# A pooled-attention and token-mixing kernel: the second batch's q transposed by transfers instead of TensorE, and alpha2 multiplied behind the transposes

## The chip, the cores and the metric

The kernel runs on one core of a Trainium2 chip. A core has TensorE (PE in the profile: matrix products and transposes by a product with the identity), VectorE (DVE), ScalarE (ACT), GpSimd (POOL) and SyncE (SP), which work through their own instruction streams and wait for each other by semaphores, and 16 engines for transfers. The metric is the device time of one execution in microseconds. Transfers issued by GpSimd appear in the profile as queue q0, those of SyncE as q1.

## What is computed

The inputs are q, k and v of 8 batches, 8 heads, 576 rows and 64 columns, all float32. First an attention in which k and v are averaged over groups of 8 rows, so that each of the 576 queries sees 72 keys:

```python
k_p = k.reshape(B, H, Sp, pool, D).mean(axis=3)      # 576 rows -> 72
v_p = v.reshape(B, H, Sp, pool, D).mean(axis=3)
scores = scale * np.matmul(q, k_p.transpose(0, 1, 3, 2))
attn = softmax(scores)
x = np.matmul(attn, v_p)          # heads side by side: (8, 576, 512)
```

Then a block that mixes rows and then columns:

```python
a1 = alpha1 * x + beta1
tok = np.einsum('ts,bsd->btd', w_tok, a1)
u = x + lam * tok
a2 = alpha2 * u + beta2
ch = np.maximum(a2 @ w_ch1, 0.0) @ w_ch2             # 512 -> 2048 -> 512
out = u + lam * ch
```

## The kernel before

The eight batches go through a software pipeline. Each batch has 576 rows, cut into four chunks of 128 and a rest of 64; the rests of two batches make one chunk together, so there are 36 chunks, worked on in nine blocks of four. While block n is in the two large products (`mlp_A`, L849, and from the third block on `product`, L972), the attention and the row mixing of batch n + 1 run between them.

The order of the work is written by hand. For batch 0 and the first half of block 0 the calls simply stand in their order (from L994 on). From then on every piece of a block has a due time in a list, `todo`, which is sorted (L1205) and emitted in that order; all engines get their instructions in the order of emission. There is no scheduler behind it.

The steps that matter here:

- **Warm-up.** `keep_warm` (L788) issues matrix products of zeros, 13 of 512 columns at L999, before q of batch 0 has landed.
- **q transposed.** The scores need q with the head's columns on the partitions. `att_F` (L575) makes two tiles `qT` per batch, one for heads 0 to 3 and one for heads 4 to 7. For batches 0 and 1 it does so on TensorE, four transposes of 128x128 (L589) for each half tile, and a copy out of PSUM (L596). From batch 2 on it is one transposing transfer per tile, issued by SyncE (L584). `att_S4` (L689) reads the tiles: the first group of four heads reads `qT[0]`, the second `qT[1]`.
- **Loads of batch 1.** q of batch 1 (`load_q_bf`), k (`load_k`, issued by GpSimd for this batch), the weights `w_ch1` in three pieces (`load_w1`), v (`load_v32`, tiles `v_main` and `v_rest`) and `w_ch2` in four pieces (`load_w2`) all go through GpSimd's queue in the first 40 us. `sum_v` (L316) adds up v on VectorE, `first_V` (L651) reads the sums.
- **Row mixing.** `mix_T` (L794) makes five products for a chunk, adds x on VectorE (L805), giving `u`, and makes a bf16 copy `u_bf`. For batch 0 this copy is multiplied by alpha2, spread over all partitions in `al2_bc` (L811, by GpSimd for chunks 0 and 2 and by VectorE for 1 and 3). For later batches it is a cast on ScalarE (L809), as alpha2 has been multiplied into `w_ch1` by then.
- **Spread alpha2.** `load_al2` (L484, called at L1032) loads alpha2 to all 128 partitions through SyncE's queue, 256 KB.
- **u transposed.** `mix_uT` (L813) transposes `u_bf` of block 0 on TensorE (L825) and copies it out of PSUM on ScalarE (L827) into `u_fm[0]`; later blocks use transposing transfers (L820).
- **First product.** For block 0, `mlp_A` (L849) runs in two halves of 256 rows: the first half needs chunks 0 and 1, the second half chunks 2 and 3.
- **Row sums.** `setup_rowsum` (L522) makes five products that put the sums of the rows of `w_tok` where beta1 needs them; the fifth call stands at L1182 with due time 6.2.

## Time and profile before

| | us |
|---|---|
| median of three runs | 332.82 (332.25 to 332.84) |
| the profiled execution | 332.3 |
| its span, first to last instruction | 330.6 |
| TensorE busy | 324.9 (98%) |
| VectorE busy | 235.5 (71%) |
| ScalarE busy | 175.5 (53%) |
| GpSimd busy | 95.6 (29%) |

The page's fourth part follows the work that ended last back to the start, and gives the share of each engine and line. Its fifth part lists groups of instructions: line, engine, operation, what it writes and reads, the shape, how many, then busy time and mean duration, then the idle time of the engine ahead of them and what ended it. The timeline has the same, in order of time: start, duration, engine, line. In a group of pipelined matrix products the sum of durations is more than the time they take, and the chain shows how far they advance. The transfer view gives, for each queue, packets, megabytes and the time that the packets took as a share of the 16 engines, which can be above 100% where packets overlap. TensorE is at its granted clock of 1.000 over the whole span.

### The profile page before, as it was taken

To read this page: it belongs to the slowest core of one execution; us is meant where nothing else is said; L and a number is where in the kernel's file an instruction comes from. 1 tells how busy PE (TensorE), PEld (TensorE's weight loads), DVE (VectorE), ACT (ScalarE), POOL (GpSimd) and SP (SyncE) were. 2 spreads that over 40 slices of the span, in tenths; PEclk is the share of its full clock that TensorE was granted. 3 is DMA by queue.
4 is the path that set the end of the run, shared out by engine and by line. 5 is a ranking of instruction groups with operands and counts; after the bars stand their busy time and mean duration, and the time that the engine had idled before them with its cause. 6 is when DMAs were issued, how large, how long until landed. Compare 5 with 4: busy or idle time off the path is not lost.

```text
span 330.6 us, 6522 instructions
## 1 busy us (share of the span) xinstructions
PE 324.9 (98%) x2528; PEld 208.9 (63%) x2528; DVE 235.5 (71%) x490; ACT 175.5 (53%) x322; POOL 95.6 (29%) x110
## 2 busy tenths in 40 slices
PE   8999999999999999999999999999999999999995
PEld 3667764455545576656775677557755866586584
DVE  6674389999589969776967796878688783265263
ACT  2775989458323852387128812782268225803710
POOL 8769738301256011700290028102610200000000
PEclk9999999999999999999999999999999999999999
DMA  8999999959894982499549934995340044003003
GB/s 119 193 219 270 268 210 249 207 145 124 165 255 68 221 203 59 76 227 165 164 119 201 171 125 89 207 195 157 65 136 2 0 65 143 2 0 129 2 32 97
DMA packets 66618, 45.83 MB, mean 139 GB/s; under 512 B 34541, under 2 KB 57205, under 8 KB 66586
## 3 DMA queue, kind: packets, MB, share of 16 engines
q1 hardware_dynamic: 52236, 32.67, 42.6%
q0 software_dynamic: 13824, 12.40, 22.9%
q8 instruction: 20, 0.33, 0.4%
q10 hardware_dynamic: 526, 0.34, 0.3%
q14 instruction: 12, 0.10, 0.1%
HBM read 38.30 MB, written 9.44 MB: 144 GB/s over the span
## 4 chain that ended last, share of the span: by engine, by line
PE 98%; DVE 1%; issue 0%; ACT 0%
PE ps_h L849 38%; PE ps_w L972 26%; PE ps_tok L801 12%; PE ps_ch L869 8%; PE ps_av L743 3%; PE ps_s L700 2%; PE ps_warm L792 2%; PE ps_kp L632 1%; PE ps_r L707 1%; PE ps_av L747 1%; PE ps_q L589 1%; PE ps_sc L680 0%; PE ps_rs L528 0%; PE ps_w L516 0%; PE ps_uT L825 0%; PE ps_v L659 0%
## 5 line engine op out<-in xcount | busy, mean ns | idle before, releaser
L849 PE MATMUL ps_h<-u_fm,w 128*128 128x512 bf16 (+2 forms) x608 | 133.7, 369 | 0.2 <-DVE bias_cols L852 0.2
L856 ACT ACTIVATE H<-ps_h,bias_cols 128x512 bf16<-128x512 f32 x144 | 98.1, 688 | 56.5 <-PE ps_h L849 55.5
L849 PEld LDWEIGHTS <-w 128*128 128x128 bf16 x608 | 65.8, 114 | 49.7 <-issue 2.2
L972 PEld LDWEIGHTS <-H 128*128 128x128 bf16 x560 | 53.4, 98 | 10.9 <-DVE u_sb L990 1.2
L809 ACT CAST u_bf<-u_sb 128x512 bf16<-128x512 f32 x32 | 19.8, 618 | 70.0 <-issue 39.9
L972 PE MATMUL ps_w<-w_l,H 128*128 128x256 bf16 x448 | 53.6, 273 | 0.0
L990 DVE TENSOR_TENSOR u_sb<-u_sb,ps_w 128x512 f32<-128x512 f32 x54 | 36.3, 682 | 17.0 <-PE ps_w L972 17.0
L765 POOL TENSOR_TENSOR xs<-x_tm,lamal_bc 128x512 bf16<-128x512 f32 x12 | 15.9, 1330 | 108.8 <-DVE x_tm L751 108.6
L801 PE MATMUL ps_tok<-xs,wtT 128*128 128x512 bf16 (+3 forms) x200 | 44.9, 381 | 0.1
L805 DVE TENSOR_TENSOR u_sb<-x_tm,ps_tok 128x512 f32<-128x512 f32 (+1 forms) x40 | 27.3, 683 | 9.9 <-PE ps_tok L801 9.9
L751 DVE TENSOR_TENSOR x_tm<-ps_av,recs 128x320 f32<-128x320 f32 x64 | 31.5, 492 | 2.6
L729 ACT ACTIVATE ET<-ps_s 72x512 f16<-72x512 f32 x56 | 32.3, 591 | 0.0
L801 PEld LDWEIGHTS <-wtT 128*128 128x128 bf16 (+3 forms) x200 | 17.4, 100 | 16.2 <-issue 1.1
L749 DVE RECIPROCAL recs<-ps_av 128x5 f32<-128x5 f32 x64 | 12.1, 188 | 16.7 <-PE ps_av L747 16.6
L670 DVE TENSOR_TENSOR v_u<-v_u 72x1024 f32<-72x1024 f32 (+1 forms) x24 | 22.7, 948 | 0.2
L972 PE MATMUL ps_w<-w_t,h_s 128*128 128x256 bf16 x168 | 22.6, 273 | 0.0
L869 PEld LDWEIGHTS <-H 128*128 128x128 bf16 x128 | 11.9, 98 | 13.7 <-issue 0.4
L372 POOL TENSOR_TENSOR k_raw<-k_raw 128x512 f32<-128x512 f32 x14 | 18.7, 1338 | 1.2 <-PE ps_ch L869 0.7
L972 PEld LDWEIGHTS <-h_s 128*128 128x128 bf16 x168 | 16.4, 98 | 4.1
L941 DVE TENSOR_TENSOR H<-H,H 128x1024 bf16<-128x1024 bf16 x14 | 9.7, 690 | 12.8 <-ACT H L856 12.7
L374 POOL TENSOR_TENSOR k_bf<-k_raw 128x512 bf16<-128x512 f32 x14 | 18.5, 1318 | 1.1
L743 PEld LDWEIGHTS <-ET 72*128 72x128 f16 x256 | 14.0, 97 | 6.0 <-DVE vp L664 0.3
(153 smaller groups left out, 369.3 us busy)
## 6 DMA issues: line engine op xcount, KB each, us to landing
out_dram<-u_sb SPq DMA_DIRECT2D x29, 256.0 KB
k_raw<-in_k_dram SPq DMA_DIRECT2D x12, 512.0 KB
v_u<-in_v_dram SPq DMA_DIRECT2D x12, 512.0 KB
q_bf<-in_q_dram POOLq DMA_DIRECT2D x16, 256.0 KB, 7.4
w<-in_moe_w_ch_dram POOLq DMA_DIRECT2D x6, 512.0 KB, 12.9
out_dram<-u_sb SPq DMA_DIRECT2D x11, 128.0 KB
w<-in_moe_w_ch_dram POOLq DMA_DIRECT2D x1, 1024.0 KB, 14.3
k_raw<-in_k_dram POOLq DMA_DIRECT2D x2, 512.0 KB, 16.7
```

The lines of the kernel that those rows point to most:

```text
L670: nc.vector.tensor_tensor(out=out, in0=t[:, :, 0:width], in1=t[:, :, width:2 * width], op=ALU.add)
L729: nc.scalar.activation(out=o, in_=i, func=AF.Exp, bias=0.0, scale=0.125)
L743: nc.tensor.matmul(out=av[:, odd + c, :], lhsT=ET[:, m0:m0 + 128], rhs=vp1[:, h % 4, :])
L751: nc.vector.tensor_tensor(out=x[:, 1 - odd:6 - odd, dd:dd + D], in0=av[:, :, 0:64], in1=rec.unsqueeze(2).to_broadcast((P, 5, D)), op=ALU.mult)
L801: nc.tensor.matmul(out=ps_tok[p0:p1], lhsT=wtT[0:kk, at, P * c:P * c + p1 - p0], rhs=xs_pool[i][0:kk, sc, :], start=(sc == 0), stop=(sc == 4))
L805: nc.vector.tensor_tensor(out=s["u"][p0:p1, :], in0=x[p0:p1, 1 + c if c < 4 else 5 - 5 * i, :], in1=ps_tok[p0:p1, 0:DM], op=ALU.add)
L809: nc.scalar.copy(out=s["u_bf"], in_=s["u"])
L849: nc.tensor.matmul(out=ps_h[:, t0:t1 + one], lhsT=w1_of(cc, j), rhs=rhs, start=(cc == 0), stop=(cc == 3))
L856: nc.scalar.activation(out=H4[n, j // 4][:, j % 4, :], in_=ps_h, func=AF.Relu, bias=bias_cols[:, j:j + 1], scale=1.0)
L869: nc.tensor.matmul(out=ps, lhsT=H_of(n, j)[:, 128 * m:128 * m + 128], rhs=(w2l if n else w2)[j // 4][:, j % 4, :], start=(j == 0), stop=(j ...
L972: nc.tensor.matmul(out=ps, lhsT=stat(j), rhs=moving(j), stop=(j == 7), start=(first and (pp == 0 or alone) and j == 0), skip_group_check=True)
L990: nc.vector.tensor_tensor(out=o, in0=o, in1=banks[key, "both"], op=ALU.add)
```

## The change

- `att_F` uses transposing transfers from batch 1 on. The two transfers for batch 1 stand right behind `mix_T(0, 3)`; the four TensorE steps in `todo` are gone.
- `mix_T` casts `u_bf` on ScalarE for every batch. `mix_uT` multiplies by alpha2 on the way out of PSUM: chunks 0, 2 and 3 by one VectorE instruction with `al2_cols` (one value per partition and group of 128 columns), chunk 1 by four ScalarE activations of 128 columns.
- `load_al2` and the tile `al2_bc` are gone; a later tile that had used its memory gets memory of its own.
- `load_w1(1)` moves up between the two `load_k` of batch 1. `mix_uT((0, 0))` moves ahead of `setup_rowsum(3)`. `setup_rowsum(4)` moves ahead of the second halves of `mlp_A`.
- The 13 warm-up products of 512 columns become 24 of 64 columns and 9 of 512.

```diff
-        if b > 1:
+        if b:
             if r == 0:
                 nc.sync.dma_start_transpose(out=st["qT"][u],
                                             in_=st["q"][u].rearrange("p h c d -> p (h c d)"))
             return
...
-        if b:
-            nc.scalar.copy(out=s["u_bf"], in_=s["u"])
-        else:
-            eng.tensor_tensor(out=s["u_bf"], in0=s["u"], in1=al2_bc, op=ALU.mult)
+        nc.scalar.copy(out=s["u_bf"], in_=s["u"])
...
-        nc.scalar.copy(out=u_fm[blk][:, :, at // 2, 128 * (at % 2):128 * (at % 2) + 128],
-                       in_=ps_uT[:, 0:512].rearrange("p (c t) -> p c t", t=128))
+        o = u_fm[0][:, :, at // 2, 128 * (at % 2):128 * (at % 2) + 128]
+        i = ps_uT[:, 0:512].rearrange("p (c t) -> p c t", t=128)
+        if at != 1:
+            nc.vector.tensor_tensor(out=o, in0=i, op=ALU.mult,
+                                    in1=al2_cols.unsqueeze(2).to_broadcast((P, 4, 128)))
+            return
+        for cc in range(4):
+            nc.scalar.activation(out=o[:, cc], in_=i[:, cc], func=AF.Copy, bias=0.0,
+                                 scale=al2_cols[:, cc:cc + 1])
...
-    for u in range(2):
-        load_k(1, u, queue=nc.gpsimd)
-    keep_warm(13)
+    load_k(1, 0, queue=nc.gpsimd)
+    load_w1(1)
+    load_k(1, 1, queue=nc.gpsimd)
+    keep_warm(24, 64)
+    keep_warm(9)
...
-    load_al2(nc.vector)
...
-    load_w1(1)
...
-    mix_T(0, 0, nc.gpsimd)
+    mix_T(0, 0)
...
     mix_T(0, 1)
+    mix_uT((0, 0))
     setup_rowsum(3)
-    mix_T(0, 2, nc.gpsimd)
+    mix_T(0, 2)
     load_v32(1)
-    mix_uT((0, 0))
     mix_uT((0, 1))
     mix_T(0, 3)
+    att_F(1, 0)
+    att_F(1, 2)
     load_w2(0)
     load_w2(1)
...
     mlp_A(0, 3, 0, 256)
+    setup_rowsum(4)
     for j in range(4):
         mlp_A(0, j, 256, 512)
...
-            for hp in range(4):
-                todo.append((2.6 + 0.9 * hp, lambda hp=hp: att_F(b, hp)))
...
-            todo.append((6.2, lambda: setup_rowsum(4)))
```

More of the change, by code (lines that the diff above doesn't have):

```diff
@@ L388, in direct @@
     lamal_bc = const.tile([P, DM], FP, tag="lamal_bc", name="lamal_bc")
-    al2_bc = const.tile([P, DM], FP, tag="al2_bc", name="al2_bc")
     b2row = const.tile([8, P], FP, tag="b2row", name="b2row")
@@ L482, in more_constants @@
         nc.vector.memset(wtT[:, :, S:640], 0.0)
-    def load_al2(behind):
-        behind.memset(al2_bc[:, 0:1], 0.0)
-        nc.sync.dma_start(out=al2_bc, in_=moe_alpha2.unsqueeze(0).to_broadcast((P, DM)))
     def spread_lam():
@@ L786, in chunk_of, with keep_warm, mix_T @@
         return key, st2[key]
-    def keep_warm(count):
-        ps = psB.tile([P, DM], FP, tag="ch", bufs=2, name="ps_warm")
+    def keep_warm(count, n=DM):
+        ps = psB.tile([P, DM], FP, tag="ch", bufs=2, name="ps_warm")[:, 0:n]
         for _ in range(count):
-            nc.tensor.matmul(out=ps, lhsT=warm[:, 0:P], rhs=warm)
-    def mix_T(b, c, eng=nc.vector):
+            nc.tensor.matmul(out=ps, lhsT=warm[:, 0:P], rhs=warm[:, 0:n])
+    def mix_T(b, c):
         key, s = chunk_of(b, c)
@@ L917, in weight_sum @@
             wino["S2"] = [const.tile([P, 4, HALF], BF, tag=tag, name="h_s")
-                          for tag in ("early", "al2_bc")]
+                          for tag in ("early", "h_s")]
             wino["S3"] = [const.tile([P, 4, HALF], BF, tag="lam_bc", name="h_s"),
```

## The prediction, as put on record before the result was known

> **What bounds the kernel now.** I read the page's chain first, then the chain in order of time, then the timeline of the first 46 us engine by engine, then the transfers.

> ```profile
> PE 98%; DVE 1%; issue 0%; ACT 0%
> 29.56 0.17 DVE bias_cols L852
> 29.75 1.92 PE ps_h L849 x16
> 31.68 0.45 PE ps_q L589 x8
> 32.56 0.22 PE ps_q L589 x4
> 33.66 0.22 PE ps_q L589 x4
> ```

> TensorE is the chain. The q transposes of the second batch are on it: 0.45 + 0.22 + 0.22 = 0.89 us, 16 at 56 ns. A microsecond taken from TensorE is a microsecond won, unless it must wait. So I looked for what could make it wait: evictions around the first mixing, and transfers, because the changed lines load both.

> ```profile
> 23.77 1.26 POOL L811 TENSOR_TENSOR u_bf<-u_sb,al_bc 128x512 bf16<-128x512 f32 x1 [1.68 <-DMA al_bc<-in_moe_alpha_dram]
> 27.48 0.95 POOL L308 DMA_DIRECT2D v_main<-in_v_dram  x1
> 40.19 0.68 DVE L324 TENSOR_TENSOR v_main<-v_main 128x512 f32<-128x512 f32 x1
> 38.73 0.30 PE L700 MATMUL ps_s<-qT,kp 64*72 64x256 bf16 x2
> 44.33 0.30 PE L700 MATMUL ps_s<-qT,kp 64*72 64x256 bf16 x2
> ```

> These are the spread load that goes (POOL waits for it, but TensorE has other work), a load with little slack (v_main lands 12.3 us after issue, at 39.8), and the first readers of the two q tiles of the second batch, 38.7 and 44.3 us. The transposes by transfer would have to land before those. Next, the transfer view in four windows: 24 to 29 us, 26 to 46, 26 to 48, and 83.6 to 86.9, where two q transposes (SyncE, issued from 82.94) move alone; then 142.5 to 145.

> ```profile
> q0 software_dynamic: 756, 1.20, 88.9%
> q1 hardware_dynamic: 597, 0.31, 27.2%
> ...
> q0 software_dynamic: 2171, 4.92, 107.4%
> ...
> q0 software_dynamic: 2406, 5.30, 107.0%
> ...
> q1 hardware_dynamic: 2091, 0.52, 82.3%
> ...
> q0 software_dynamic: 563, 0.28, 91.0%
> q1 hardware_dynamic: 369, 0.10, 39.1%
> ```

> The columns are packets, MB and share of the 16 engines. Two q transposes are some 2,050 packets of 256 bytes and need 3 us alone. But GpSimd's queue (q0) is never empty from 5 to 54 us, and beside it SyncE's queue (q1) got 597 packets against 756: about one for one, whatever the size of q0's packets (in 27 to 28 us it is 72 against 79, and those are of 3.7 KB). So rem_raw's 256 KB, issued by 22.3 us, were moving until 29. The last pair is the one place where a DMA transpose (u_fm, issued at 138.78) meets q0: 369 against 563.

> **The change part by part**, against the profiled execution's own 332.3 us (span 330.6; the median of three runs is 332.8).

> *Warm-up.* Thirteen 512-column products become 24 of 64 and 9 of 512. The 13 advance by 0.427 us each (weight loads at 1.79, 2.22, 2.64 ...), 5.55 us; those after 6.9 us take 0.22 on the chain, so the clock doubles around 6.8. Nine cost 3.84. A 64-column product costs 29 ns warm (att_K: 16 in 0.47), so 59 ns cold: 24 cost 1.4. Sum 5.25, 0.3 less. q has landed by 6.14 (issue 1.34 + 4.8), but the transposes would then begin while the clock is still halved and give about 0.1 back: I take -0.2. Bounds: -0.7 (start bound by q's landing) and +1.9 (if each small product pays its weight load's 0.15 us: 24 x 0.15 + 3.84 - 5.55).

> *alpha2 behind the transposes, rowsum(4) moved up.* Now u_bf is a plain ScalarE cast (0.62, row L809), and alpha2 is applied by VectorE (L805's kind, 0.68) for chunks 0, 2, 3, and by four ScalarE activations for chunk 1. Bounds of one of these: 0.29 (by the lines of 128x256, 0.39, and 128x512, 0.585) advancing 0.19 each, or 0.16 (the 128x4 copy); I take 0.29, the nearer. In the times of before: mix_T(0,2) leaves TensorE at 25.6; VectorE adds until 26.5; ScalarE casts until 27.1 and only then, in its order, scales chunk 1 until 27.9. The first mlp_A needs that: it ends at 28.0 instead of 27.4. The last transpose, behind two mlp_A, ends at 29.5; VectorE scales chunk 3 from 29.55 to 30.23. So the second halves start at 30.26, where before they start at 29.75: +0.5. rowsum(4) (5 x 29 ns) now lies in that wait: -0.15. Bounds: +0.1 (VectorE's scaling and ScalarE's four at 0.16) and +1.1 (nothing overlaps).

> *q by transfer.* -0.89 on TensorE, and four ScalarE copies of 0.6 less, which lay beside TensorE. SyncE is free from 22.3 to 36.4 us, so the issues (1.3 us each) cost nothing; the wtT copies behind them are read only from 53 us. The transfers need landed q (before: 10.16 + 15.4 = 25.6).

> *al2_bc's load left out, load_w1(1) ahead of load_k(1,1).* 256 KB less for the engines: in 21 to 22 us q0 fell to 0.12 MB from 0.21, in all about 0.7 us. The transposes take 1.75 us of engine time (2,050 packets at the 1,173 a us of 64 to 65 us). So q0's loads behind them, v_main too, are later by up to 1.0. The moved load makes k_raw(1,1) 2.5 us later (land 30.9 to about 34); its sum is due on POOL at 34.4 and read by TensorE at 39.4: hidden.

> Without a wait for a transfer: -0.2 + 0.5 - 0.15 - 0.89 = -0.75, 331.55.

> *When do the transposes land?* First packet 1.1 us after issue (82.94, 84.0), so 26 us. Packets of q1 per packet of q0: 0.66 by the u_fm row, 0.79 by the loads' row, 1.0 by al2_bc's (76 against 79 in 21 to 22 us). I take 0.9, between the last two: the loads do not keep all engines supplied, and the transposes spread evenly. The first tile then needs 1,140 packets of q0: about 34 us, in time for 38.0. Both need 2,280: q0 has moved 2,171 by 46 and 2,406 by 48, so 46.9, and 47.9 with the 1.0 above. TensorE reaches att_S4(1,1) at 44.33 - 0.75 = 43.6 and waits 4.3. Sum: 332.3 - 0.75 + 4.3 = **335.9**. At 1.0 the wait is 1.4 (333.0; 2,052 packets by 44), at 0.79 it is 6.3 (337.8), at 0.66 about 9 (340.6).

> [...]

> **The rivals.**

> *The transposes get through* (faster; the opposite sign). They decide at att_S4(1,1): with 1.1 packets or more per q0 packet, 2,050 are done before 43 us. For it: in 144 to 145 us, as q0 runs out, they pass it (308 against 154). Against it: every stretch with q0 full. Then 331.55, if v_main is in time too.

> *v_main is late instead.* Same, but 2,050 packets early push v_main from 39.8 to 40.8. VectorE's sums start 0.6 later, first_V and att_AV(1,0) have 0.4 of slack: +0.2 on before, 332.5; bounds 332.0 to 333.3 (delay 0.5 to 1.8).

> [...]

> *The transposes starve*: in 142.5 to 143.5 us they moved 15 packets against q0's 253. If they only move when q0 is dry, at 54 us, both readers wait: 332.3 - 0.75 + 16.5 = 348.

> **How the numbers follow.** Late second tile 0.45 (333 to 340.6), v_main late 0.22 (half of it above 332.97), through 0.23, starved 0.10. About 0.2%, 0.66 us, is what a measurement here can tell from no change. Faster: nearly all of the third, 0.23. Same: half of the second and the rest, 0.13. Slower 0.64. The range runs from 331.3 to 340.5; the likeliest case's own is 333 to 340.

> **What would show it.** Right: a gap in TensorE before att_S4's second group of ps_s products, near 44 us, released by the qT transfer, with q1's packets trailing q0's until 46 to 48. Also ps_h starting near 30.1 rather than 29.75, no L589 row after 14 us, and the warm-up ending near 6.7. Wrong: q1 showing some 2,000 packets between 26 and 31 us; then no gap at 44, and VectorE's L324 tells which of the two rivals it is. A warm-up of over 6 us would mean that small products pay for their weights.

## The result, and the profile after

The changed kernel takes 346.70 us (median of 5 runs, 345.94 to 347.58), the kernel before 332.82 beside it (332.18 to 332.96). The ratio is 1.0405, with a 95% interval of 1.0366 to 1.0444. Slower was right, the size was not: I had said 335.9, with a range to 340.5. The profiled execution took 345.9 us, its span is 344.1, 13.5 more than before. One remark for what follows: in one experiment's profile (the one with small packets) TensorE ran at half clock from 11.07 to 24.72 us (granted clock 0.55 on average from 10 to 20 us, 0.76 from 20 to 30), so distances there are counted from the second halves of the first product.

The chain that ended last, and the list of TensorE's waits (in total, times, longest):

```profile
PE 83%; DMA 13%; POOL 3%; issue 0%; DVE 0%; POOLq 0%
...
PE ps_s L695 <- DMA qT<-q_bf: 9.5, 2, 8.3
...
```

TensorE was 98% of the chain; now 13% of the span hangs on transfers. The timeline of TensorE, the rows that answer to those shown of before (line numbers have moved by a few: the products of `att_S4` are L695 now):

```profile
30.59 4.56 PE L848 MATMUL ps_h<-u_fm,w 128*128 128x256 bf16 x40 [0.20 <-DVE u_fm L822]
...
39.76 0.30 PE L695 MATMUL ps_s<-qT,kp 64*72 64x256 bf16 x2 [1.17 <-DMA qT<-q_bf]
...
44.88 0.30 PE L654 MATMUL ps_v<-vs,pool_v 128*72 128x256 f16 x1 [0.91 <-DVE vs L325]
...
55.70 0.42 PE L695 MATMUL ps_s<-qT,kp 64*72 64x256 bf16 x2 [8.29 <-DMA qT<-q_bf]
...
61.06 1.03 PE L868 MATMUL ps_ch<-w,H 128*128 128x512 bf16 x4
```

In the kernel before these stand at 29.75, 38.73, 42.77, 44.33 and 47.50; the third and the last of them are

```profile
42.77 0.27 PE L659 MATMUL ps_v<-vs,pool_v 128*72 128x256 f16 x1
...
47.50 1.03 PE L869 MATMUL ps_ch<-w,H 128*128 128x512 bf16 x4
```

So all of the 13.5 us is lost by 61.06 (13.56 there), and it divides like this:

| stretch | us | from |
|---|---|---|
| warm-up and first mixing | +0.84 | 30.59 against 29.75 |
| q transposes gone (0.89), rowsum(4) moved (0.15) | -1.04 | |
| first q tile late | +1.2 | wait of 1.17 |
| v late | +2.05 | TensorE is ready for the second scores at 47.41 (55.70 less 8.29), 3.08 late; 1.03 of it was there at 39.76 |
| second q tile late | +8.29 | its wait |
| half clock behind the wait | +2.2 | 55.70 to 61.06 takes 5.36, before 3.17 |

VectorE's sums of v wait for their load:

```profile
43.67 0.69 DVE L324 TENSOR_TENSOR v_main<-v_main 128x512 f32<-128x512 f32 x1 [2.36 <-DMA v_main<-in_v_dram]
```

The table's last line shows in the clock. Busy time in two stretches: their length, then PE, PEld, DVE, ACT and POOL with their counts of instructions, then the granted clock, the share of the transfer engines and GB/s:

```profile
50.00:55.00 5.00, 0.00 (x0) 0.00 (x0) 0.00 (x0) 0.00 (x0) 0.00 (x0) 0.58 1.63 94
55.00:60.00 5.00, 4.30 (x29) 2.33 (x30) 1.93 (x5) 1.88 (x5) 1.78 (x2) 0.50 1.23 297
```

And the transfers: packets, MB and share of the 16 engines in 28 to 46 and 50 to 54 us.

```profile
q0 software_dynamic: 1555, 3.76, 95.7%
q1 hardware_dynamic: 1448, 0.37, 16.5%
...
q0 software_dynamic: 274, 0.25, 82.9%
q1 hardware_dynamic: 287, 0.07, 79.4%
```

By the sizes of the packets in the trace, 1,391 of q1's in the first stretch are the transposes' (256 bytes each), against 1,555 of q0's, whose mean is 2.4 KB. From 30 us on it is one for one: 1,258 against 1,293 until 46 us, 335 against 334 from 46 to 50, 287 against 274 in the last. But q0 itself is slower than in the trace of before, where it moved 1,953 packets from 28 to 46 us. And from 50 to 54 us both queues all but stand: 70 packets a us each, at 80% of the engines' time. That stretch was the puzzle.

### The profile page after: what moved, and what is told of

Read it like the earlier page. It is cut to its first block, busy times and chain, and to the rows that moved or that the text cites. A ratio compares the mean times of both kernels' runs of the same rounds, so it can differ in the third digit from the quotient of the medians.

```text
span 344.1 us, 6527 instructions
## 1 busy us (share of the span) xinstructions
PE 326.7 (95%) x2532; PEld 209.5 (61%) x2532; DVE 237.4 (69%) x490; ACT 175.7 (51%) x322; POOL 93.2 (27%) x108
## 4 chain that ended last, share of the span: by engine, by line
PE 83%; DMA 13%; POOL 3%; issue 0%; DVE 0%; POOLq 0%
PE ps_h L848 34%; PE ps_w L971 25%; PE ps_tok L796 10%; DMA qT<-q_bf 9%; PE ps_ch L868 8%; DMA q_bf<-in_q_dram 4%; PE ps_s L695 2%; PE ps_av L738 2%; PE ps_r L702 1%; POOL q_bf L266 1%; PE ps_av L742 0%; POOL v L300 0%; PE ps_kp L627 0%; POOL k L272 0%; POOL w L550 0%
## 5 line engine op out<-in xcount | busy, mean ns | idle before, releaser
L848 PE MATMUL ps_h<-u_fm,w 128*128 128x512 bf16 (+2 forms) x608 | 135.2, 372 | 0.7 <-ACT u_fm L826 0.5
L803 ACT CAST u_bf<-u_sb 128x512 bf16<-128x512 f32 x36 | 22.3, 619 | 72.2 <-issue 39.6
L744 DVE RECIPROCAL recs<-ps_av 128x5 f32<-128x5 f32 x64 | 12.1, 189 | 27.2 <-PE ps_av L742 27.1
L796 PEld LDWEIGHTS <-wtT 128*128 128x128 bf16 (+3 forms) x200 | 17.4, 100 | 16.5 <-issue 1.1
L695 PE MATMUL ps_s<-qT,kp 64*72 64x256 bf16 x112 | 11.4, 287 | 9.5 <-DMA qT<-q_bf 9.5
```

Of the source, the lines that this page charges most:

```text
L796: nc.tensor.matmul(out=ps_tok[p0:p1], lhsT=wtT[0:kk, at, P * c:P * c + p1 - p0], rhs=xs_pool[i][0:kk, sc, :], start=(sc == 0), stop=(sc == 4))
L803: nc.scalar.copy(out=s["u_bf"], in_=s["u"])
L848: nc.tensor.matmul(out=ps_h[:, t0:t1 + one], lhsT=w1_of(cc, j), rhs=rhs, start=(cc == 0), stop=(cc == 3))
```

## The experiments

All times are medians, the ratio is to the kernel before in the same session.

### Which part of the change costs

Theory T: the two transposing transfers hold nearly all of the loss. Rival M: the new mixing, or the moved loads, hold a part. First the change without the transfers:

```diff
-        if b:
+        if b > 1:      # and the four att_F steps back in todo
```

> The changed kernel with the second batch's q transposed on TensorE again (at the places of the kernel before); all else of the change stays. Theory T (the transposing transfers hold nearly all of the 13.5 us): the two waits (1.2 and 8.3 us), the halved clock behind the second (2.2 us) and the late v_main (1.2 us) go, 0.89 us of TensorE comes back; what stays is the later mixing (second halves 0.84 us later, less 0.15 for rowsum(4)): 332.8 + 0.7 = 333.5, between 332.8 and 334.2. Rival M (the mixing, the loads left out or moved hold a part too): above 335.

333.19 us, 1.0029 (1.0004 to 1.0055): T holds. TensorE in its profile no longer waits for a tile:

```profile
39.23 0.30 PE L695 MATMUL ps_s<-qT,kp 64*72 64x256 bf16 x2
...
44.84 0.30 PE L695 MATMUL ps_s<-qT,kp 64*72 64x256 bf16 x2
```

Also, v_main, issued at 21.04, lands 17.5 us later, at 38.5; in the changed kernel it was issued at 22.08 and took 21.6, to 43.7.

Then the transfers alone in the kernel before:

```diff
-        if b > 1:
+        if b:
...
     mix_T(0, 3)
+    att_F(1, 0)
+    att_F(1, 2)
```

> The kernel before with only the two transposing transfers, issued at the place of the changed kernel; alpha2, its spread load, the warm-up, load_w1(1) and rowsum(4) stay as before. Theory T: the second tile lands when GpSimd's queue has moved as many packets as the tile pair has, about 54 to 55.5 us of the profile whatever TensorE does, so the end is that of the changed kernel: 345 to 347.5. Rival M: below 343, the other parts being the rest.

345.69 us, 1.0380 (1.0353 to 1.0406). T again: the whole loss without any other part of the change. The waits are 3.32 and 9.35 us in its profile, which is of the longest of its four executions (347.98).

```profile
41.18 0.30 PE L700 MATMUL ps_s<-qT,kp 64*72 64x256 bf16 x2 [3.32 <-DMA qT<-q_bf]
...
57.86 0.43 PE L700 MATMUL ps_s<-qT,kp 64*72 64x256 bf16 x2 [9.35 <-DMA qT<-q_bf]
```

The two small parts, each alone in the kernel before. Warm-up:

```diff
-    keep_warm(13)
+    keep_warm(24, 64)
+    keep_warm(9)
```

> The kernel before with only the warm-up of the changed kernel (24 products of 64 columns and 9 of 512 in place of 13 of 512). By the traces the first transposes start 0.42 us earlier (6.46 in place of 6.88): 332.2, between 331.9 and 332.5. Rival: the 0.4 us is swallowed by a later wait for a load, 332.6.

332.56 us, 1.0003 (0.998 to 1.0025): nothing that can be measured. The first transposes start at 6.48 here, at 6.88 in the trace of before, but at 5.97 in the next kernel, which has the old 13 products. The start moves by 0.9 us between executions, more than the edit is worth, so my reading of 0.42 us from two traces was no evidence.

Alpha2 behind the transposes, its load out, rowsum(4) moved, with the old warm-up and order of loads:

```diff
-    load_al2(nc.vector)
...
-            eng.tensor_tensor(out=s["u_bf"], in0=s["u"], in1=al2_bc, op=ALU.mult)
+        nc.scalar.copy(out=s["u_bf"], in_=s["u"])
...
+            nc.vector.tensor_tensor(out=o, in0=i, op=ALU.mult,
+                                    in1=al2_cols.unsqueeze(2).to_broadcast((P, 4, 128)))
```

> The kernel before with alpha2 multiplied behind the transposes and its spread load left out, rowsum(4) and the order of the first mixing as in the changed kernel; q on TensorE, warm-up and the order of k and w1 loads as before. From milestones: second halves 1.26 us later than with the old path and the old start, rowsum(4) 0.15 back: 332.6 + 1.1 = 333.7, between 333.2 and 334.2. Rival (my forecast of this part, +0.35): 333.0.

333.53 us, 1.0019 (1.0004 to 1.0034), 0.6 us. In the traces the stretch from the second chunk's products (22.81 before, 23.05 here) to the second halves (29.75, 30.86) takes 6.94 and 7.81 us: 0.87 more, 0.15 of it given back by rowsum(4).

### Half of the transfers

Only the first tile by transfer, the second on TensorE:

```diff
-        if b:
+        if b > 1 or b and u == 0:      # and two att_F steps back in todo
```

> The changed kernel with the transfer only for the first q tile (1,024 packets); the second is transposed on TensorE again. Theory P: the first tile lands as in the changed kernel (wait of 0.5 to 1.5 us before the first scores, at 39 to 40 us); q1 is empty from then on, so v_main is later than without transposes by about half as much (late by 0 to 1 us for VectorE); no wait of 8 us, no fall of the clock: 332.6 + 0.6 (as measured with all on TensorE) - 0.45 + 1 + 0.5 = 334.2, between 333.2 and 335.3. Rival S (a transfer beside GpSimd's queue waits until that is dry): the first tile lands after 46 us, 340 or more.

335.17 us, 1.0078 (1.0048 to 1.0109), within P's range, near its upper end. The wait for the tile is 0.38 us, shorter than expected, and with 1,024 packets fewer nothing waits 8 us.

### What the tiles wait for: packets or bytes

Theory P: SyncE's queue gets one packet for each packet of GpSimd's queue. Rival S: it gets a share of bytes or time, or only what is left over. The test keeps bytes and loads and changes the size of packets:

```diff
-            out=w2[g], in_=moe_w_ch2[...].rearrange("(p i) d -> p i d", i=4))
+            out=w2[g], in_=moe_w_ch2[...].rearrange("(i p) d -> p i d", i=4))
...
-        return t[...].rearrange("p c (m i) -> p c i m", i=4)[:, cc, j % 4, :]
+        return t[...].rearrange("p c (i m) -> p c i m", i=4)[:, cc, j % 4, :]
```

> The changed kernel with w2 read in rows of one line each (row i*128+p to partition p, place i, in place of row 4p+i; the hidden units are taken in the matching order from w1), so that GpSimd's queue moves the same bytes in up to four times as many, smaller packets. Theory P (SyncE's queue gets one packet for each packet of GpSimd's queue): 2,048 transposing packets pass in half the time or less, the second tile lands at 42 to 47 us in place of 54.5, the wait of 8.3 us shrinks to 0 to 3 us and the clock does not fall: 334 to 338. Rival S (the share is one of bytes or engine time, or the transposes only move when the other queue is dry): the second tile lands at 53 to 56 us as before, 345 to 348.

336.06 us, 1.0098 (1.0070 to 1.0125): three quarters of the loss gone by smaller packets on the other queue. From the first to the last transposing packet it is 18.6 us, against 26.5 in the changed kernel. The profile is of the longest of the five executions (340.13). The transfer view from 42 to 50 us:

```profile
q0 software_dynamic: 1148, 1.14, 90.4%
q1 hardware_dynamic: 1152, 0.29, 35.4%
```

And the second scores in TensorE's timeline:

```profile
50.79 0.30 PE L695 MATMUL ps_s<-qT,kp 64*72 64x256 bf16 x2 [2.07 <-DMA qT<-q_bf]
```

From the second halves (34.74) to these scores it is 16.05 us, against 25.11 in the changed kernel and 14.58 before. S falls. Two details of P's expectation did not come: the second tile landed at 50.8 in this profile, not by 47, and the clock did fall behind the wait of 2.07 us (0.51 from 52 to 54 us).

The transfers by themselves, with no computation:

```python
for name, form in (("w_4KB", "(p i) d -> p i d"), ("w_1KB", "(i p) d -> p i d")):
    for g in range(4):
        load(g, form, name)            # as load_w2
    release(nc.gpsimd.tensor_copy)     # writes an element of each q tile
    pair("qT_" + name)                 # two transposing transfers by SyncE
    for g in range(4, 12):
        load(g, form, name)
```

> No part of the reference is computed (the output is filled with zeros); only transfers run, in four stages one behind the other. 1: the pair of q transposes (2,048 packets) alone. 2: the pair beside twelve loads of w2's size and form on GpSimd's queue (packets of 4 KB, four issued ahead). 3: the same with the rows laid out as in the run with small packets (packets of 1 KB). 4: the pair beside loads of 16 KB into one partition each, issued by ScalarE, which use few of the 16 engines or one. Theory P (a packet for a packet): stage 1 takes about 3 us; in stage 2 the packets of SyncE's queue equal those of GpSimd's (within 5%) until that is done: 1,536 packets at some 55 a us, so the pair lands after 25 to 30 us; in stage 3 both queues move some 150 packets a us and the pair lands after 11 to 15 us, before the loads end. Rival B (a share of bytes or of time): stages 2 and 3 take equally long. Stage 4, for the slow stretch: if the transposing packets advance in step over the engines, so that one lagging engine holds all (theory L), the pair's packets trickle at well under 300 a us from the first on as long as the one-partition loads run; if each engine goes its own way (theory I), 1,800 of 2,048 have moved within 3 us, the rest later.

The stages did not come one behind the other as planned: the stores of the zeros stood ahead of the first pair in SyncE's queue, and the loads did not wait for it. So the landing times can't be used, but the rates can. From 40 to 46 us (8-KB stores against 4-KB loads), 56 to 60 (transposes against 4-KB loads) and 64 to 72 (transposes against 1-KB loads):

```profile
q0 software_dynamic: 172, 0.63, 51.8%
q1 hardware_dynamic: 170, 1.25, 51.5%
...
q0 software_dynamic: 204, 0.73, 94.3%
q1 hardware_dynamic: 198, 0.05, 12.0%
...
q0 software_dynamic: 1250, 1.25, 91.8%
q1 hardware_dynamic: 1253, 0.31, 30.2%
```

A packet for a packet three times, whichever side has the larger ones: the stores got twice the bytes of the loads, the transposes a quarter (beside 1 KB) or a fourteenth (beside 4 KB). Beside 4 KB the transposes made 50 packets a us, beside 1 KB 157, as P had it (55 and 150); B falls. In the last stage, beside one-partition loads, the pair took 6.0 us and 1,402 packets moved in the first 3: neither of the two numbers expected there.

### The clock

```diff
+            if first and u:
+                todo.append((at - 0.01, lambda: keep_warm(34)))
             todo.append((at, lambda u=u: att_S4(b, u)))
```

> The changed kernel with 34 idle 128x128x512 products (7.3 us at the full clock) on TensorE right ahead of the second group of scores, where it waits 8.3 us. Theory C (the halved clock behind the wait costs 2.2 us): the granted clock stays at 1.00 through 50 to 60 us and the end comes 2 us earlier: 344.5, between 344 and 345.2. Rival N (the clock does not fall because of the wait, or what runs there at half speed is off the chain): 346.2 to 347.2.

343.96 us, 1.0347 (1.0320 to 1.0375), against 1.0405 (1.0366 to 1.0444); the intervals overlap and the median is 0.04 us under C's range, but the profile is clear. The clock, same stretches as above:

```profile
50.00:55.00 5.00, 3.73 (x27) 1.80 (x25) 0.00 (x0) 0.00 (x0) 0.00 (x0) 1.00 1.56 135
55.00:60.00 5.00, 4.95 (x49) 2.73 (x47) 4.19 (x12) 4.51 (x9) 3.50 (x3) 1.00 1.18 310
```

From the second scores (54.46) to the first ps_ch products (57.38) it takes 2.92 us, in place of 5.36. C holds: some 2 us of the loss are the clock and not the wait.

### What else makes the second tile late

The transposing packets start at 28 us, not at 26. I thought that rem_raw's loads, ahead of them in the queue, were the reason, and moved these to GpSimd's queue.

```diff
-    load_rem(1, behind=nc.vector)
+    load_rem(1, nc.gpsimd, nc.vector)
```

> The changed kernel with the loads of the second batch's rem_raw (256 KB) moved from SyncE's queue to GpSimd's, so that nothing stands ahead of the transposes in their queue. Theory P (packet for packet from the first packet on): the first transposing packet moves at 26 instead of 28.5 us, the first tile lands by 37 (no wait of 1.2 us before the first scores), the second some 2 us earlier than in the changed kernel, and the end with it: 344 to 345.5. Rival E (the second tile lands when GpSimd's queue has run out, whenever the transposes began): 346 to 347.5.

347.82 us, 1.0461 (1.0428 to 1.0493), above both ranges. My reason falls. The transposes were issued at 24.35, and with nothing ahead of them SyncE's queue still moved no packet from 25 to 28 us, while GpSimd's moved 561; the first transposing packet started at 28.28.

So 3.9 us pass from issue to first packet beside a full queue, where it was 1.2 alone (82.94 to 84.15 in the trace of before); what takes them isn't shown. The move also held up GpSimd: v_main was issued at 27.45, and in this profile TensorE waits 3.27 us for GpSimd's xs and 4.2 us for the sums of v. So its end tells nothing on the two theories.

For the slow stretch of 50 to 54 us I tried to take away what moved beside it, first by issuing the third batch's q loads later:

```diff
-                    at = {1: 11.0, 2: 6.5}.get(b, 0.4) + 0.1 * u
+                    at = {1: 17.0, 2: 6.5}.get(b, 0.4) + 0.1 * u
```

> The changed kernel with the third batch's q loads (two of 256 KB, small packets) issued behind the first att_X of batch 1 on GpSimd, some 20 us later, so that GpSimd's queue runs dry when w2 has landed, at 48 to 49 us. In the changed kernel 1,405 of the 2,048 transposing packets had moved by 46 us, some 1,500 by 48.5; from 50 to 54 us the packets of both queues took 0.14 to 0.18 us each. Theory Q (the meeting with the small packets of q makes that slow stretch): with the queue dry the last 500 packets need 0.5 to 1.5 us, the second tile lands at 49.5 to 51, the wait is 2 to 4 us, 340 to 342.5. Rival W (transposing packets are slow there by themselves, as in the stretch of 38.5 to 42 us with the w2 loads held back, where they took 0.06 us and more each with little else moving): the second tile lands at 52 to 55 us, 344 to 347.

344.90 us, 1.0369 (1.0327 to 1.0411), wait 7.70 us: W. With hardly any packets left on GpSimd's queue the transposes still crept; 49 to 53 us:

```profile
q1 hardware_dynamic: 465, 0.16, 101.3%
q0 software_dynamic: 59, 0.19, 23.8%
```

Then by keeping the w2 loads back until the second tile has landed (their early calls are left out, and two of VectorE's passes over w2 come later):

```diff
+            hold = const.tile([P, 1], BF, tag="hold", name="hold")
+            todo.append((10.5, lambda: nc.gpsimd.tensor_copy(out=hold, in_=st1[1]["qT"][1][:, 0, 0:1])))
+            for g in range(4):
+                todo.append((10.6 + 0.1 * g, lambda g=g: load_w2(g)))
```

> The changed kernel with GpSimd's queue emptied for the transposes: GpSimd reads one element of the second transposed tile before it issues the four w2 loads, so that they start when the tile has landed; the VectorE passes that read w2 early are due later. Theory P (SyncE's queue is held to the packet rate of GpSimd's queue, and runs at its own rate when that is dry): GpSimd's queue runs dry when v_main and v_rest have landed, 40 to 43 us, the second tile lands within 2 us after that, by 45; the wait of 8.3 us goes to 0 to 1.5 us and the clock stays up. w2's first part is read at 48 to 50 us and has 2.5 us for each part from its issue: at most 2 us of waiting. 332.8 to 336. Rival S (the tiles need the time whatever else moves: slow in themselves): the second tile lands at 50 us or later, w2 behind it, 345 or more.

338.94 us, 1.0190 (1.0156 to 1.0224), between P's range and S's. The second tile lands by 43.2 us, as P said, and nobody waits for it. But the first lands hardly sooner, at 42.3, where it was 39.7 in the changed kernel; its reader waits 3.37 us, and the clock is at half for 3.4 us behind that (0.56 on average from 42 to 45 us, 0.87 from 45 to 48). By then 1,024 packets had long moved (38.4); what held the landing isn't shown. Transfers from 38 to 42 and 42 to 43 us:

```profile
q1 hardware_dynamic: 780, 0.19, 101.1%
q0 software_dynamic: 82, 0.25, 20.7%
...
q1 hardware_dynamic: 485, 0.16, 63.7%
```

As long as a few of q0's packets (82 of 3 KB on average) were left, the transposes made 195 a us and filled the engines' time (101.1%); with q0 empty, 485 packets moved in one microsecond. That gave theory L, an idea that no run had shown: the transposing packets of a tile advance in step over the 16 engines, and an engine that still has big packets to move holds all the others. Rival I: each engine goes its own way.

```python
for i in range(64):
    if i == 8:
        pair("qT_one")                 # released by ScalarE here
    nc.scalar.dma_start(out=junk[i:i + 1, :], in_=flat[:, 4096 * i:4096 * i + 4096])
```

> No part of the reference is computed (the output is filled with zeros); only transfers run. Stage 1: the pair of q transposes (2,048 packets) alone, for the rate that the forecast took from one microsecond of the trace of before (1,173 a us); expected 570 to 1,170 packets a us and 2 to 4 us. Stage 2: the pair beside 64 loads of 16 KB into one partition each (128 packets of 8 KB, which took 0.34 us each in the run before and lie on one engine, or few), eight of them issued ahead. It tells two theories of the slow stretch apart (640 packets in 8 us with GpSimd's queue nearly run out, and the same with the w2 loads held back). L, the transposing packets advance in step over the 16 engines, so that the engine with big packets left holds all: they trickle at 30 to 100 a us, evenly, from the first to the last, and the pair takes 20 us or more. I, each engine goes its own way: 1,900 packets move in the first 4 us and the rest, some 130, trickle behind at a few a us.

Alone, the pair needs 2.8 us (6.7 to 9.5; 730 packets a us), as expected. Beside the one-partition loads it needs 3.9 us (11.6 to 15.5), so L's 20 us did not come, nor I's slow rest, because the loads are single packets of 16 KB, 0.61 us each and only about one a us. But what such a packet does can be seen. One starts at 12.67; from 12.50 to 12.90, and from 12.90 to 13.30 us:

```profile
q1 hardware_dynamic: 282, 0.07, 270.9%
q10 hardware_dynamic: 1, 0.02, 9.5%
...
q1 hardware_dynamic: 2, 0.00, 9.6%
```

A single packet of another queue, and within 0.3 us the transposes all but stop: 282 packets in 0.4 us, then 2. The same happens with the next one (464 packets from 13.60 to 14.00, 2 from 14.16 to 14.56). By the single packet records, 21 or 22 transposing packets of 256 bytes last 0.59 to 0.75 us in each of these two stops, where the median is 18 ns, and they end 0.2 and 0.3 us after the big packet does. A third big packet, under way from 11.18 to 12.42, let them run until 12.2 us and slowed them until 12.6.

By I they would not all but stop; by L they would, so beside 16-KB packets these two stops speak for L. Whether it is the big packet's engine that holds them or the one partition that it writes was not separated. That L makes the slow stretch of the changed kernel is an inference: there, from 50 to 54 us, long packets (over 0.15 us) hold 88% of the transposes' packet time, while on average 2.6 of q0's 4-KB packets are under way. But 10.9 of q0's 512-byte packets are too, and these last 0.18 us each, where it was 0.06 in the trace of before. Issuing these later did not help (W, above), so they alone are not the reason; what held the packets there stays open.

No kernel tried was measurably faster than the one before.

## Why the prediction was wrong, step by step

**Warm-up, -0.2.** Not measurable (0.998 to 1.0025). Harmless, but read from too few executions. The doubling of the clock around 6.8 us was right: the pace of the products goes from 0.427 to 0.22 us there, and the first record of a granted clock, of 1.00, begins at 6.84 us in the trace of before and at 6.43 in the changed kernel's. No record covers what lies ahead of it, so the 1.000 for the whole span is not shown for the first 6.84 us.

**Alpha2, +0.5, and rowsum(4), -0.15.** +0.87 in the traces, +0.6 us in time for both (0.1 to 1.1), within the bounds. ScalarE's four scalings took 1.14 us, where I had 0.86 (0.29 and three more at 0.19).

**q on TensorE, -0.89.** Right.

**The engine-time cost, "later by up to 1.0".** Wrong: v_main landed at 43.7, against 38.5 with q on TensorE, 5.2 us later. I had charged the transposes with their own 1.75 us of engine time. Alone they took 2.8 us, and beside q0 they cost it far more than that; by what way was not shown. I had v_main late as a rival of its own, at 0.2 us; it came on top and cost 2.05.

**When the transposes land: the step that failed.** "First packet 1.1 us after issue, so 26 us" was 28.4. The ratio, "I take 0.9", was right: from the first to the last transposing packet 2,048 moved against 2,231 of q0's, which is 0.92, and the forecast's 2,280 is near that. What failed is the time that q0 needs for so many, "q0 has moved 2,171 by 46 and 2,406 by 48", and the 1.0 us added for the transposes' own load on it. These counts come from a trace in which q0 ran without the transposes. In the changed kernel it had moved, from 26 to 46 and from 26 to 48 us:

```profile
q0 software_dynamic: 1836, 4.08, 94.9%
...
q0 software_dynamic: 1944, 4.48, 95.1%
```

Counted from 28.4 us on, q0 moves 2,231 packets by 48.4 in the trace of before, by 47.7 in the one with q on TensorE and the loads in the new order, and by 55.0 in the changed kernel. So the term of 1.0 us measured 6.6 or more. The tile landed at 55.7, 7.8 us behind the 47.9. The reader came later too (47.4, not 43.6), so that the wait is 8.29 in place of 4.3. The first tile, forecast for 34 us and "in time for 38.0", landed at 39.7 and cost 1.2. SyncE needed 8.1 us for the second issue, not 1.3, but no engine waited for that.

Put together, the profile's 13.5 us against the forecast 3.55: 0.55 more in the stretches without a wait, 1.2 for the first tile, 2.05 for v, 4.0 for the second tile and 2.2 for the clock. The kind of wait and its place were forecast; of the 10 us that are missing, some 5.5 are in terms that the sum did not have.

**The clock.** The sum had no term for it, and it cost 2.2 us behind the wait of 8.29. The granted clock is 0.50 from 50.8 to 61.0 us. It also fell behind shorter waits: 3.32 us with the transfers alone (0.79 on average from 41 to 44 us, 0.64 from 44 to 47), and 2.07 us with the small packets, where the clock from 52 to 54 us was

```profile
52.00:54.00 2.00, 2.00 (x10) 0.86 (x9) 1.32 (x4) 0.86 (x2) 1.32 (x1) 0.51 1.23 212
```

In that last profile the clock had also fallen once, at 11.07 us, with no wait ahead of it (the last one before it in TensorE's timeline is of 0.16 us, at 7.00). So that the 2.07 us caused the second fall is likely and not shown.

**The rivals.** "Get through" and "v_main late instead" fell with the one-for-one turns (1,880 transposing packets against q0's 1,901 from 30 to 54 us). "Starve" gave 348, near the time, by another way: the first tile landed at 39.7, long before q0 was dry, and the second moved one for one all along.

## What to carry to other kernels

Here a transposing transfer of 256-byte packets beside a queue of large loads was paid in the other queue's packets, not in bytes (2,048 against 2,231): count how many packets the full queue moves until the reader comes, and take that count from a trace with the transposes in it, because they slowed that queue too (2,231 packets took 26.5 us in place of 20). With transposes at 56 ns each on TensorE, 0.89 us of it was far cheaper than 2,048 packets at the wrong time. A wait put into a chain that TensorE carries also cost clock behind it: 2.2 us behind the wait of 8.29, nothing behind the one of 1.17 (granted clock 1.00 from 40 to 44 us).
